# Moving the SBUF tiles of a clustered-attention and MLP kernel by up to 608 bytes

## Chip, cores and metric

The kernel runs on one core of one Trainium2 chip. The metric is the device time of one execution in microseconds (us); the median of three runs of the kernel before is 843.01 us (842.73 to 843.17).

## What is computed

The reference is an attention with a mask by cluster, followed by two MLPs. All arrays are float32.

```python
q_assign = argmax(einsum('bhsd,hcd->bhsc', q_n, c_n), -1)   # likewise k_assign, 16 clusters
mask = q_assign[:, :, :, None] == k_assign[:, :, None, :]
scores = where(mask, scale * q @ k.T, -1e9)
x = softmax(scores) @ v                    # batch 2, heads 8, sequence 768, head dim 64
x = x.transpose(0, 2, 1, 3).reshape(1536, 512)
h = x @ w_in                               # 512 -> 2048
x = where(h > 0, h, exp(min(h, 0)) - 1) @ w_out          # 2048 -> 512
return ((x @ w_a) * (x @ w_b)) @ w_out2    # 512 -> 1536 -> 512
```

## The kernel before, in words

**Order.** The order of all work is written out by hand in the string ORDER; each word names a small function (an op) and its arguments, and every engine runs its share in that order. The first 270 us are mostly attention, the next 40 us a mixture, and the rest is MLP alone.

**Attention.** For each of 16 heads (batch times heads) and each of six tiles of 128 queries, `sc` (L671) makes the scores in PSUM with float32r matmuls of 384 columns: two with `qa`/`ka` (128 rows, the float32 values in two parts) and two with `qb`/`kb` (80 rows, 16 of which carry the mask). `rm` (L679, VectorE) takes the maximum, `ex` (L690, ScalarE) the exponential into `pf` and its row sums into `sum`. `tr` (L723) transposes `pf` on TensorE with `pf` as stationary operand and the identity `identf` as moving one; `th` and `tl` cut the result into two float16 parts in `pt`, or POOL's `hi` and `lo` and a transposing DMA `td` do. `av` (L782) multiplies `pt` with the float16 parts `v1`, `v2` of v. `ra`, `rc`, `rx`, `rb` (L742, L747, L753, L763) spread the reciprocal of the row sums with `identf` as moving operand. `sm` (L571) makes the similarities to the centroids from `cq1`, `ck1`, `ck2`, `cq2`, and `st` (L585) transposes them from `sim`.

**MLP.** The 1536 tokens go in three chunks c of 512, the hidden width in blocks blk of 512. Every product of two float32 matrices is three float32r matmuls of 128 rows, 128 stationary and 512 moving columns (`mm3`, L921 to L923): high by high, high by low, low by high part. There are four kinds of op, each of 24 such matmuls (the very last `o` is cut in two of 12):

- `h:blk.c.fp`, 24 ops (4 blocks, 3 chunks, 2): weights `w[2 blk]` stationary, `x_c` moving.
- `x2:blk.c.dp`, 24 ops: weights `w[2 blk + 1]` stationary, the activation `g` moving.
- `ab:blk.c.ft`, 36 ops (3 blocks, 3 chunks, 4): weights `w[8 + 3 blk]` for 12 matmuls, then `w[9 + 3 blk]` for 12, stationary; `x_c` moving.
- `o:blk.c.jp`, 18 ops: `g` stationary, weights `w[10 + 3 blk]` moving.

That makes 102 ops and 2448 matmuls. Each matmul has its own weight load (PEld), which starts with the matmul before it. VectorE's `gl` (L992) and `pl` (L1039) write the low part of `g` that `x2` and `o` need. POOL's `wq` (L907) writes the last part of each weight tile.

**Where tiles lie.** SBUF is filled from two ends: pools opened with `left(...)` grow upward, pools with `right(...)` downward from the top. A tile takes its bytes per partition, rounded up to 32, and tiles of a pool lie in the order of their creation. Weight tile `w[i]` goes to pool `w(i % 4)`; the activation tile of step u = 3 blk + c (counted on over the four `h` blocks and the three `ab` blocks) goes to `gA` for even and `gB` for odd u. In the compiled program the MLP's operands begin at these places, all tiles being multiples of 512 bytes long:

| tiles | side | first byte | modulo 512 |
|---|---|---|---|
| w0 | left | 50176 | 0 |
| x0 | left | 66560 | 0 |
| w1 | left | 82944 | 0 |
| gA | left | 107520 | 0 |
| x1 | left | 123904 (to 140288) | 0 |
| x2 | right | 155616 (to 172000) | 480 |
| gB | right | 180192 | 480 |
| w2 | right | 196576 | 480 |
| w3 | right | 212960 (to 229344) | 480 |

In the attention (modulo 512): `qa`, `ka`, `qb`, `kb` 224; `pf`, `pt` 416; `v1`, `v2` 416 or 160; `rx` 480; `identf` 160; `cq1` and its like 352; `sim` 96; `identb` 0. `sum` and `rs` take 32 bytes a buffer, two buffers each; `desc` takes 64 and `ohscale` 32.

The lines that the change touches are L294 (the first right-hand pool), L310 to L316 (the constants), L688 (`sum`) and L741 (`rs`).

Of the kernel before, what the change touches and what calls it, by code (L numbers as in the profile page):

```python
# [10 lines left out]
F32 = mybir.dt.float32  # L11
# [10 lines left out]
P = 128  # L22
B, H, S, D, C = 2, 8, 768, 64, 16
# [232 lines left out]
def clustered_attention_moe_kernel(  # L256
# [21 lines left out]
    def left(name, reuse="tile", under=ctx):  # L278
        return under.enter_context(tc.tile_pool(name=name, bufs=1, reuse_waits=reuse))

    def right(name, under, reuse="tile"):
        return under.enter_context(
            tc.tile_pool(name=name, bufs=1, side="right", reuse_waits=reuse)
        )

    const = left("const")
# [4 lines left out]
    wp = left("wp")  # L291
    ectx, actx, actxA, actxB = ExitStack(), ExitStack(), ExitStack(), ExitStack()
    ep = left("prep", under=ectx)
    ap = right("attn", actx)  # L294
    spB = right("operandsB", actxB)
    sp = [right("operandsA", actxA), spB]
# [2 lines left out]
    def take(pool, tag, shape, dt, name, bufs=1):  # L299
        return pool.tile(shape, dt, tag=tag, bufs=bufs, name=name)  # L300
# [6 lines left out]
    identb = ep.tile([P, P], BF16, name="identb")  # L307
    warm = ep.tile([P, 512], BF16, name="warm")
    nc.vector.memset(warm, 0.0)
    eps = const.tile([P, 1], F32, name="eps")  # L310
    nc.vector.memset(eps, 1e-9)
    identf = const.tile([P, P], F32, name="identf")
    make_identity(nc, identf)
    desc = ep.tile([P, C], F32, name="desc")
    ones = ep.tile([NH, P], F32, name="ones")
    ohscale = ep.tile([64, 2], F32, name="ohscale")  # L316
    cn = ep.tile([P, D], F32, name="cn")
    nc.sync.dma_start(out=cn, in_=cent)
    csq = ep.tile([P, D], F32, name="csq")
# [156 lines left out]
    pairs = [{} for _ in range(NPAIR)]  # L476

    def flat(t):
        return t.rearrange("p t d -> p (t d)")
# [203 lines left out]
    @op  # L683
    def ex(g, t):
        j, x = divmod(g, 2)
        f, a = divmod(t, 3)
        if (x, a) == (0, 0):
            pairs[j]["sum", f] = take(ap, "sum", [P, 2, 3], F32, f"sum_{j}_{f}", 2)  # L688
        pf = st[g][f"pf{t}"] = take(ap, "pf", [P, S], F32, f"pf{t}_{g}", 3)
        nc.scalar.activation(  # L690
            pf.rearrange("p (a b) -> p a b", a=2), st[g].pop(f"sc{t}")[:, :, :HALF], AF.Exp,
            bias=st[g].pop(f"nm{t}"), accum_out=pairs[j]["sum", f][:, x, a : a + 1],
        )
# [44 lines left out]

    @op
    def ra(j, f):  # L740
        s = pairs[j]["rs", f] = take(ap, "rs", [P, 6], F32, f"rs_{j}_{f}", 2)  # L741
        nc.scalar.activation(s, flat(pairs[j]["sum", f]), AF.Identity, bias=eps)  # L742

    @op
# [345 lines left out]
    for word in ORDER.split():  # L1090
        name, args = word.split(":")
# [45 lines left out]
```

## Time and profile before

| | |
|---|---|
| median of three runs | 843.01 us |
| span of the profiled execution, first to last instruction | 842.1 us |
| TensorE busy in the span | 823.9 us, 98% |
| VectorE, ScalarE, POOL busy | 609.5, 408.3, 357.5 us |
| granted TensorE clock | 1.00 in every stretch |

The profiled execution's own time is not told beside its span; the span is 0.9 us under the median of the runs. A matmul's end is modelled in these records, its start is not: two matmuls overlap in the table of busy time, so the pace of TensorE is read from start to start.

### The profile page before, as it was taken

How to read it: one execution, taken by the hardware profiler on the slowest of the kernel's cores; microseconds unless marked ns; L12 is line 12 of the kernel's file. 1: busy time of each engine (PE TensorE's matmuls, PEld its weight loads, DVE VectorE, ACT ScalarE, POOL GpSimd, SP SyncE). 2: the span in 40 equal slices, each digit the busy share in tenths (PEclk: the TensorE clock that was granted, in tenths of full speed). 3: DMA queues.
4: the chain of work that ended last, by engine and by line, in shares of the span. 5: the costliest groups of instructions: out<-in, count | busy, mean ns of one | idle time of the engine just before them, and what ended most of it. 6: DMA issues, size and time to landing. Idle time of an engine off the chain costs nothing.

```text
span 842.1 us, 12217 instructions
## 1 busy us (share of the span) xinstructions
PE 823.9 (98%) x4626; PEld 656.1 (78%) x4626; DVE 609.5 (72%) x871; ACT 408.3 (48%) x730; POOL 357.5 (42%) x307
## 2 busy tenths in 40 slices
PE   9899999999999999999999999999999999999998
PEld 8777666776667888888888888888888888888886
DVE  5898998899889879698687688776247874455222
ACT  6687877877787644454454365342122332222020
POOL 3666776687472325354444443332034440422000
PEclk9999999999999999999999999999999999999999
DMA  9446655666343212222222222113002221110102
GB/s 280 111 91 147 134 100 108 132 126 105 65 86 64 75 58 69 75 76 94 82 89 82 80 76 76 51 50 100 1 3 97 61 85 56 51 51 0 51 1 100
DMA packets 65626, 68.12 MB, mean 81 GB/s; under 512 B 49888, under 2 KB 49888, under 8 KB 65568
## 3 DMA queue, kind: packets, MB, share of 16 engines
q1 hardware_dynamic: 65328, 66.76, 30.6%
q8 instruction: 36, 0.59, 0.3%
q10 hardware_dynamic: 240, 0.59, 0.3%
q14 instruction: 22, 0.18, 0.1%
HBM read 48.27 MB, written 3.15 MB: 61 GB/s over the span
## 4 chain that ended last, share of the span: by engine, by line
PE 90%; DVE 4%; POOL 3%; ACT 2%; issue 2%; POOLq 0%; ACTq 0%; DVEq 0%
PE ab L923 8%; PE ab L922 8%; PE ab L921 8%; PE sc L671 6%; PE h L921 5%; PE h L923 5%; PE h L922 5%; PE x L923 5%; PE x L921 5%; PE x L922 5%; PE av L782 4%; PE o L923 4%; PE o L921 4%; PE o L922 4%; PE tt L723 4%; PE sm L571 4%
## 5 line engine op out<-in xcount | busy, mean ns | idle before, releaser
L679 DVE TENSOR_REDUCE nm<-sc 128x1 f32<-128x768 f32 x96 | 90.9, 950 | 14.3 <-PE sc L671 13.6
L690 ACT ACTIVATE pf<-sc,nm 128x768 f32<-128x768 f32 x96 | 86.8, 905 | 21.0 <-DVE nm L679 13.2
L1023 ACT COPY t0ab<-ab 128x512 f32<-128x512 f32 x36 | 21.1, 587 | 113.7 <-PE ab L923 113.7
L732 DVE TENSOR_TENSOR pt<-tt,pt 128x384 f16<-128x384 f32 x132 | 69.3, 547 | 5.5 <-ACT pt L727 5.1
L1028 DVE TENSOR_TENSOR t1ab<-ab,t0ab 128x512 f32<-128x512 f32 x36 | 24.8, 689 | 66.0 <-ACT t0ab L1023 65.9
L727 ACT CAST pt<-tt 128x384 f16<-128x384 f32 x126 | 57.3, 479 | 25.8 <-PE tt L723 24.3
L671 PE MATMUL sc<-ka,qa 128*128 128x384 f32 x192 | 58.2, 384 | 7.1 <-ACT pf L690 6.5
L723 PE MATMUL tt<-identf,pf 128*128 128x128 f32 x396 | 60.3, 277 | 4.1 <-DVE pt L732 2.0
L723 PEld LDWEIGHTS tt<-identf,pf 128*128 128x128 f32 x396 | 45.7, 140 | 15.1 <-issue 4.3
L782 PE MATMUL av<-pt,v 128*64 128x384 f16 x576 | 54.0, 329 | 0.0
L852 ACT ACTIVATE wg<-wraw 128x512 f32<-128x512 f32 x68 | 45.1, 667 | 17.9 <-DMA wraw<-in_w_out_dram 7.2
L705 POOL TENSOR_TENSOR phl<-pf,phl 128x768 f16<-128x768 f32 x30 | 50.9, 1696 | 4.7 <-issue 1.9
L869 DVE SCALAR_TENSOR_TENSOR wf<-wraw,wg 128x512 int32<-128x512 int32 x68 | 51.2, 753 | 1.9
L882 DVE SCALAR_TENSOR_TENSOR wg<-wraw,wg 128x512 f32<-128x512 uint32 x68 | 49.7, 731 | 1.8
L671 PE MATMUL sc<-kb,qb 80*128 80x384 f32 x192 | 49.5, 339 | 0.0
L1039 DVE TENSOR_TENSOR gl<-t1ab,gh 128x512 fp32r<-128x512 f32 x36 | 33.8, 940 | 18.8 <-ACT gh L1034 18.6
L857 DVE TENSOR_SCALAR wg<-wg 128x512 f32<-128x512 f32 x68 | 40.1, 590 | 6.4 <-ACT wg L852 6.4
L671 PEld LDWEIGHTS sc<-ka,qa 128*128 128x128 f32 x192 | 28.8, 189 | 19.8 <-ACT pf L690 13.6
L782 PEld LDWEIGHTS <-v 128*64 128x64 f16 x576 | 29.7, 109 | 17.6 <-issue 6.9
L862 DVE TENSOR_SCALAR wg<-wg 128x512 int32<-128x512 int32 x68 | 41.8, 615 | 2.1
L698 POOL CAST phl<-pf 128x768 f16<-128x768 f32 x26 | 23.5, 903 | 43.9 <-ACT pf L690 42.9
L992 DVE TENSOR_TENSOR gl<-t1h,gh 128x1024 fp32r<-128x1024 f32 x24 | 33.9, 1414 | 7.7 <-ACT gh L985 7.7
(388 smaller groups left out, 2349.0 us busy)
## 6 DMA issues: line engine op xcount, KB each, us to landing
wraw<-in_w_out_dram SPq DMA_DIRECT2D x28, 512.0 KB, 3.3
wraw<-in_w_in_dram SPq DMA_DIRECT2D x16, 512.0 KB, 3.7
wraw<-in_w_a_dram SPq DMA_DIRECT2D x12, 512.0 KB, 3.6
wraw<-in_w_b_dram SPq DMA_DIRECT2D x12, 512.0 KB, 3.4
rawq<-in_qt_dram SPq DMA_DIRECT2D x30, 192.0 KB, 3.6
acc<-in_v_dram SPq DMA_DIRECT2D x4, 768.0 KB, 11.1
rawk<-in_kt_dram SPq DMA_DIRECT2D x15, 192.0 KB, 3.7
kb<-ka SPq DMA_DIRECT2D x14, 192.0 KB, 3.0
```

The costliest lines, as they stand in the source:

```text
L671: nc.tensor.matmul(s[:, j, :HALF], a[:, qs], b[:, j * HALF : (j + 1) * HALF], start=i == 0, stop=i == 1,)
L679: nc.vector.reduce_max(out=nm, in_=st[g][f"sc{t}"][:, :, :HALF], axis=AX.XY, negate=True)
L690: nc.scalar.activation(pf.rearrange("p (a b) -> p a b", a=2), st[g].pop(f"sc{t}")[:, :, :HALF], AF.Exp, bias=st[g].pop(f"nm{t}"), accum_ou ...
L705: nc.gpsimd.tensor_sub(phl[:, S:], st[g].pop(f"pf{t}"), phl[:, :S])
L723: nc.tensor.transpose(tt[:, k * P : (k + 1) * P], pf[:, o : o + P], identf)
L727: (nc.vector.tensor_copy, nc.scalar.copy)[e](next(parts_of(g, t, u)), st[g][f"tt{t}{u}"])
L732: nc.vector.tensor_sub(lo, st[g].pop(f"tt{t}{u}"), hi)
L782: nc.tensor.matmul(pairs[j]["av"][x * 64 : (x + 1) * 64].rearrange("p (a q) -> p a q", a=3), st[2 * j + x][("v1", "v2")[vi]][:, kt_, :], s ...
L869: nc.vector.scalar_tensor_tensor(out=f, in0=raws[n][:, :, 1], scalar=-0x40000000, in1=g, op0=ALU.bitwise_and, op1=ALU.bitwise_or,)
L921: nc.tensor.matmul(ps, lhi, rhi, start=first, stop=False)
L922: nc.tensor.matmul(ps, lhi, rlo, start=False, stop=False)
L923: nc.tensor.matmul(ps, llo, rhi, start=False, stop=last)
```

## The change

A new pool, opened first on the right, holds one tile of 120 float32 (480 bytes) that nothing reads or writes. `identf` is created ahead of `eps`. `desc` is created twice as wide and used by half, `ohscale` with 16 columns instead of 2, `sum` and `rs` with 16 instead of 6. No instruction is added, removed or moved.

```diff
+    edge = right("edge", ctx).tile([P, 120], F32, name="edge")
     ap = right("attn", actx)
...
+    identf = const.tile([P, P], F32, name="identf")
     eps = const.tile([P, 1], F32, name="eps")
     nc.vector.memset(eps, 1e-9)
-    identf = const.tile([P, P], F32, name="identf")
     make_identity(nc, identf)
-    desc = ep.tile([P, C], F32, name="desc")
+    desc = ep.tile([P, 2 * C], F32, name="desc")[:, :C]
     ones = ep.tile([NH, P], F32, name="ones")
-    ohscale = ep.tile([64, 2], F32, name="ohscale")
+    ohscale = ep.tile([64, 16], F32, name="ohscale")
...
-            pairs[j]["sum", f] = take(ap, "sum", [P, 2, 3], F32, f"sum_{j}_{f}", 2)
+            pairs[j]["sum", f] = take(
+                ap, "sum", [P, 16], F32, f"sum_{j}_{f}", 2
+            )[:, :6].rearrange("p (x a) -> p x a", x=2)
...
-        s = pairs[j]["rs", f] = take(ap, "rs", [P, 6], F32, f"rs_{j}_{f}", 2)
+        s = pairs[j]["rs", f] = take(ap, "rs", [P, 16], F32, f"rs_{j}_{f}", 2)[:, :6]
```

## Rows read from the trace of the kernel before

**Rows 1.** The page: busy time by engine, TensorE's granted clock in 40 slices.
```profile
PE 823.9 (98%) x4626; PEld 656.1 (78%) x4626; DVE 609.5 (72%) x871; ACT 408.3 (48%) x730; POOL 357.5 (42%) x307
...
PEclk9999999999999999999999999999999999999999
```

**Rows 2.** The page: the chain of work that ended last, by engine.
```profile
PE 90%; DVE 4%; POOL 3%; ACT 2%; issue 2%; POOLq 0%; ACTq 0%; DVEq 0%
```

**Rows 3.** Who TensorE's matmuls waited for, whole span: total us, times, longest.
```profile
PE sc L671 <- ACT pf L690: 6.5, 9, 1.4
PE tt L723 <- DVE pt L732: 2.0, 4, 1.0
PE vbc L460 <- DVE vdg L453: 1.7, 1, 1.7
PE warm_ps L407 <- DVE eps L311: 1.2, 1, 1.2
PE tt L723 <- ACT pf L690: 1.2, 1, 1.2
...
PE op L626 <- DVE oht L617: 0.2, 1, 0.2
```

**Rows 4.** Timeline, TensorE, weights left, moving left: start us, us, engine, line.
```profile
412.99 0.39 PE L921 MATMUL h<-x0h,w4h 128*128 128x512 f32 x1
...
439.97 0.39 PE L923 MATMUL x<-gh,w5l 128*128 128x512 f32 x1
```

**Rows 5.** Timeline, TensorE, weights right, moving right.
```profile
374.52 0.39 PE L921 MATMUL h<-x2h,w2h 128*128 128x512 f32 x1
...
385.17 0.39 PE L923 MATMUL h<-x2h,w2l 128*128 128x512 f32 x1
```

**Rows 6.** Timeline, TensorE, weights right, moving left.
```profile
341.21 0.39 PE L921 MATMUL h<-x0h,w2h 128*128 128x512 f32 x1
...
363.38 0.40 PE L923 MATMUL h<-x1h,w2l 128*128 128x512 f32 x1
```

**Rows 7.** Timeline, TensorE, weights left, moving right.
```profile
440.19 0.40 PE L921 MATMUL h<-x2h,w4h 128*128 128x512 f32 x1
...
462.36 0.40 PE L923 MATMUL x<-gh,w5l 128*128 128x512 f32 x1
```

**Rows 8.** Timeline, TensorE, one `ab` op and the next: weights w11 right, w12 left.
```profile
650.15 0.39 PE L921 MATMUL ab<-x0h,w11h 128*128 128x512 f32 x1
...
652.95 0.39 PE L921 MATMUL ab<-x0h,w12h 128*128 128x512 f32 x1
...
655.67 0.39 PE L921 MATMUL ab<-x0h,w11h 128*128 128x512 f32 x1
```

**Rows 9.** Timeline, TensorE: first matmul of the unbroken MLP run and the last.
```profile
297.02 0.39 PE L921 MATMUL x<-gh,w1h 128*128 128x512 f32 x1
...
838.04 0.39 PE L923 MATMUL o<-w16h,gl 128*128 128x512 f32 x1
```

**Rows 10.** Groups by form, attention's matmuls: busy us, mean ns, idle before.
```profile
L723 PE MATMUL tt<-identf,pf 128*128 128x128 f32 x396 | 60.3, 277 | 4.1 <-DVE pt L732 2.0 <-ACT pf L690 1.2 <-ACT ohs L631 0.5
...
L763 PE MATMUL rbp<-identf,rx 128*128 128x128 f32 x96 | 13.6, 278 | 0.1
...
L571 PE MATMUL sm<-qa,cq 128*64 128x384 f32 x32 | 12.3, 385 | 0.2 <-DVE pt L732 0.2
```

**Rows 11.** By line: VectorE's product of `ab`, ns min/median/max over both sides' tiles.
```profile
L1028 DVE TENSOR_TENSOR t1ab<-ab,t0ab x36: 677/692/693, 546.1 to 817.0; 128x512 f32<-128x512 f32 x36
```

**Rows 12.** Timeline, VectorE: the last `gl` ahead of the `x2` of step 1.2.
```profile
393.86 1.22 DVE L992 TENSOR_TENSOR gl<-t1h,gh 128x1024 fp32r<-128x1024 f32 x1
```

**Rows 13.** Timeline, TensorE: the first matmul that reads that half of `gl`.
```profile
398.23 0.39 PE L922 MATMUL x<-gl,w3h 128*128 128x512 f32 x1
```

**Rows 14.** Timeline, POOL: the last two pieces of w15, then TensorE's first use.
```profile
733.35 2.55 POOL L907 TENSOR_TENSOR w15l<-wf,wg 128x512 fp32r<-128x512 f32 x2
...
741.96 0.39 PE L923 MATMUL ab<-x0h,w15l 128*128 128x512 f32 x1
```

## The prediction

> **What bounds the kernel now.** I read the page first. [...] So the question is where TensorE waits and how fast it goes when it does not. The waits of its matmuls are nine entries, all of the start or the attention: none names a line of the MLP (L921 to L923) [rows 3]. From 297.02 us, where the attention's last interruptions of `h` are over, to the last matmul's start at 838.04 us TensorE therefore runs one unbroken stream [rows 9]. By the program it holds all but the first four `h` ops, 2448 - 96 = 2352 matmuls, hence 2351 intervals: 541.02 / 2351 = 230.1 ns each. Anything that changes this pace goes straight to the end.
>
> The third view is the timeline of TensorE, read from start to start, sorted by the side of SBUF on which the two operands lie:
>
> - weights left, moving left: 120 matmuls, 26.98 us / 119 = 226.7 ns [rows 4];
> - weights right, moving right: 48 matmuls, 10.65 / 47 = 226.6 ns [rows 5];
> - weights right, moving left: 96 matmuls, 22.17 / 95 = 233.4 ns [rows 6];
> - weights left, moving right: 96 matmuls, 22.17 / 95 = 233.4 ns [rows 7].
>
> There are two paces only. [...] It is not the op, the weights or the chunk: inside one `ab` op, with `x0` moving throughout, the 12 matmuls with the right-hand w11 take 2.80 / 12 = 233.3 ns each and the next 12 with the left-hand w12 2.72 / 12 = 226.7 ns [rows 8].
>
> In the table of places left-hand operands begin at 0 modulo 512 and right-hand ones at 480, and all slices of them are multiples of 512 bytes. So a matmul is fast when the two addresses agree modulo 512, whatever their common value, and slow when they differ by 32 bytes.
>
> **The change part by part.** *The edge tile.* It is the first right-hand pool, so it lies on top and pushes all below it down by 480 bytes. The MLP pool follows directly: x2, gB, w2, w3 go from 480 to 0 modulo 512. Nothing of the left changes there, since the constants keep their sum and the pools behind `prep` start where `prep` starts. Every MLP pair then agrees.
>
> How many are dear now is counted from the code. `h`: even blocks have w0, dear with chunk 2; odd blocks w2, dear with chunks 0 and 1: 2 x 1 + 2 x 2 = 6 pairs of block and chunk, 12 ops. `x2`: one chunk of each block disagrees (step u of the other parity than the block): 4 pairs, 8 ops. `ab`: block 0 (w0, w1) with chunk 2, 4 ops; block 1 (w3, w0) half of each of 12 ops, worth 6; block 2 (w2, w3) with chunks 0 and 1, 8 ops; 18 in all. `o`: weights of w2, w1, w0 against g: 2 + 2 + 1 chunks, 10 ops. That is 48 ops of 24, 1152 of 2448 matmuls, 1152 x 6.67 ns = 7.7 us. From the whole run it is 541.02 - 2351 x 0.2267 = 8.0 us; the 0.3 us between the two are the matmuls just after a switch, which reach the fast pace late. With no switches left they go too, so I take **8.0 us**, with 7.7 as the lower value.
>
> *Does the faster stream stay unbroken?* Its suppliers must be early enough. `x2` and `o` need the last `gl` or `pl`; the tightest of the 21 heads is the `x2` of block 1, chunk 2: `gl` ends at 393.86 + 1.22 = 395.08 us [rows 12], the matmul that reads it starts at 398.23 us [rows 13], 3.1 us later. In between lies about one op, which shrinks by at most 24 x 6.67 = 0.16 us. Among the weights w15 is near: written at 733.35 + 2.55 = 735.90 us, first used at 741.96 us, 6.1 us [rows 14]; some 60 matmuls lie between the VectorE work that lets it go on and its use, 0.4 us of shrinking. Cost 0; what covers it is those margins, and if the `gl` cover were gone each head would pay the lateness itself. VectorE's own operations do not care: the 36 products of `ab`, half with scratch on each side, lie within 677 to 693 ns [rows 11].
>
> *The rounded small tiles and identf* act in the attention only. Edge, `rs` and `sum` together move `pf`, `pt`, `v1`, `v2` to 32 bytes less modulo 512 (416 to 384, 160 to 128), and `qa`, `ka`, `qb`, `kb` to 96 less (224 to 128); `rx` goes from 480 to 0. `identf` goes from 160 to 128. On the left `desc` and `ohscale` push `cq1` and its like from 352 to 448 and `sim` from 96 to 192. What counts by the rows above is the difference of a pair, and it stays for `sc` (0), for `tr` (416 - 160 = 256, then 384 - 128) and for `av`. It changes for 96 records of `rb` (320 to 384), 128 matmuls of `sm` (multiples of 128, then 64 past them) and 48 of `st`, 272 in all. The trace of before cannot show what the new differences cost, so the bound on both sides is the only step seen, 272 x 6.67 ns = 1.8 us. The nearest row is the transpose, whose difference is 256 and which takes 277 ns where `rb` takes 278 [rows 10]: one nanosecond, 0.1 us for all `rb`. I take 0. In the attention TensorE also has waits that take up such a gain or loss [rows 3]. `edge` issues nothing and no queue is touched: no instruction, DMA or wait is added on any engine.
>
> *Order of reuse.* Tiles wait for the earlier tiles in whose bytes they lie. Left moves by +96 and right by -480 to -608 bytes against each other; adding the sizes up, every MLP tile lies over the same attention tiles as before (`ohs` now ends on the byte where gA begins). Cost 0; otherwise `x2`'s parts, written while the attention ends, would be late.
>
> **Sum.** 842.1 - 8.0 = 834.1 us of span. The end behind the last matmul stays. The median of the runs is 0.9 us above the span, so 835.0 us. The bounds: 833.2 with all 272 attention matmuls gaining, 837.1 with all losing and 7.7 us for the MLP.
>
> **The rivals.** *A. Sides, not offsets: no change, 843.0 us.* In the trace of before offset and side go together, so the dear pairs could be those whose operands lie in two different regions. Then equal offsets give nothing. Against it: x1 ends at 140288 and x2 begins at 155616, and left-hand tiles from 50176 to 140288 pair well with each other, as do right-hand ones from 155616 to 229344 [rows 4, 5]; a border would have to fall into those 15 KB. Distance does not do it either: w0 and x1 are fast over 74 KB [rows 4], x1 and w2 slow over 73 KB [rows 6]. Chance 0.05.
> [...]
>
> *B. The shift does not come out equal: 843.0 us.* If the edge were not the topmost tile or not of 480 bytes after rounding, left and right would differ by another number. 480 is a multiple of 32 and the pool is the first on the right. Chance 0.03.
>
> *C. TensorE outruns its suppliers: slower.* Place: the 21 heads of `x2` and `o`. To end more than 0.2% slower, waits would have to eat 8.0 us and 1.7 more, 9.7 / 21 = 0.46 us at every head, beyond margins of 3.1 us and more; the result would be 844.7 us or above. It decides where a head's `gl` comes over 3.1 us later, relative to TensorE, than now. VectorE is 72% busy [rows 1], the shrinking per op is 0.16 us. Chance 0.02.
>
> *D. Half the gain: 838 to 841 us,* if the agreed pairs that I did not see (right at 0 with left at 0) behaved like neither group, or the attention paid more than its bound. Left with left at 0 is exactly rows 4. Chance 0.05.
>
> **How the numbers follow.** The forecast's own case, every MLP matmul at 226.7 ns and the attention as it is, has 0.85: 835.0 us. With D's 0.05 faster has 0.90; A and B make 0.08 for the same, C 0.02 for slower. The range is the forecast's bounds, 833.2 to 837.1 us; the rest left out is about 0.15, so no rival has to be taken in. 0.2% of 843 us, 1.7 us, is about what a measurement of this kernel can tell from no change.
>
> **What would show it.** In the changed kernel every stretch of MLP runs at 226.7 ns from start to start, also the counterparts of rows 6, 7 and both halves of rows 8; the run from the first `x2` to the last matmul takes 533 us; the waits of TensorE still name no MLP line; the first `x2` still starts near 297 us, within 2 us. The prediction is wrong if mixed pairs still take 233.3 ns (A, B), if L921 to L923 appear among the waiting lines (C), or if the MLP starts later than 299 us.

## The result

The kernel after takes 835.36 us (median of six runs, 834.66 to 838.53) against 843.09 us (842.73 to 846.54): a ratio of 0.9902, 95% interval 0.9881 to 0.9922. The profiled execution has a span of 833.1 us, 9.0 us less than before.

The page and the waits come first (the line numbers are four higher than before, L925 to L927 are `mm3`).

The page of the kernel after, busy time by engine:

```profile
PE 815.0 (98%) x4626; PEld 655.3 (79%) x4626; DVE 609.9 (73%) x871; ACT 408.4 (49%) x730; POOL 357.4 (43%) x307
```

Its waits of TensorE's matmuls, again nine entries, of which the longest and the last:

```profile
PE sc L673 <- ACT pf L694: 6.5, 9, 1.4
...
PE op L628 <- DVE oht L619: 0.2, 1, 0.2
```

As many instructions as before, the same busy times on VectorE, ScalarE and POOL to 0.4 us, the same waits. Only TensorE's busy time fell, by 8.9 us. Where, the timeline of TensorE tells (start us, us, engine, line): the unbroken MLP run [rows 9], the mixed pairs [rows 6, 7] and the `ab` op with w11 and w12 [rows 8].

```profile
296.19 0.39 PE L925 MATMUL x<-gh,w1h 128*128 128x512 f32 x1
...
339.71 0.39 PE L925 MATMUL h<-x0h,w2h 128*128 128x512 f32 x1
...
361.24 0.39 PE L927 MATMUL h<-x1h,w2l 128*128 128x512 f32 x1
...
437.63 0.39 PE L925 MATMUL h<-x2h,w4h 128*128 128x512 f32 x1
...
459.16 0.39 PE L927 MATMUL x<-gh,w5l 128*128 128x512 f32 x1
...
644.35 0.39 PE L925 MATMUL ab<-x0h,w11h 128*128 128x512 f32 x1
...
647.07 0.39 PE L925 MATMUL ab<-x0h,w12h 128*128 128x512 f32 x1
...
649.79 0.39 PE L925 MATMUL ab<-x0h,w11h 128*128 128x512 f32 x1
...
829.08 0.39 PE L927 MATMUL o<-w16h,gl 128*128 128x512 f32 x1
```

The whole run takes 532.89 us for its 2351 intervals, 226.7 ns each, where it took 541.02. Weights right with moving left is now 21.53 / 95 = 226.6 ns (233.4 before), weights left with moving right the same, and both halves of the `ab` op take 2.72 us for 12. So 8.13 of the 9.0 us come from the MLP. The run starts 0.83 us earlier, at 296.19 instead of 297.02 us, and the end behind the last matmul is 4.0 us in both (833.1 - 829.08, 842.1 - 838.04).

The 0.83 us were there before the attention began. Busy time of TensorE in the stretch from 4 to 8 us (us, busy, matmuls, granted clock, DMA share, GB/s), before and then after:

```profile
4.00:8.00 4.00, 4.00 (x51) 1.00 1.03 222
```

```profile
4.00:8.00 4.00, 4.00 (x66) 1.00 1.03 223
```

These are the warm-up matmuls of `wm`, which depend on nothing of the change. In the timeline 51 of them run at 106 ns start to start in the profiled execution before and 35 in the one after, until the pace becomes 56 ns; 16 x 50 ns = 0.8 us. All of them have one shape, 128 columns, so up to 6.7 us in the one execution and 5.0 us in the other TensorE ran at about half its later pace, although the clock column shows 1.00 for both: it does not tell the two apart, and the 1.00 in every stretch, in the table of before, does not speak for these first microseconds. Between this and the MLP the two executions stay within 0.1 us of each other: the attention gained and lost nothing.

### The profile page after: what moved, and what is told of

Same layout as the page of the kernel before. It is cut to its first block, busy times and chain, and to the rows that moved or that the text cites. A ratio compares the mean times of both kernels' runs of the same rounds, so it can differ in the third digit from the quotient of the medians.

```text
span 833.1 us, 12217 instructions
## 1 busy us (share of the span) xinstructions
PE 815.0 (98%) x4626; PEld 655.3 (79%) x4626; DVE 609.9 (73%) x871; ACT 408.4 (49%) x730; POOL 357.4 (43%) x307
## 4 chain that ended last, share of the span: by engine, by line
PE 89%; DVE 3%; POOL 3%; ACT 2%; issue 2%; DMA 0%; SPq 0%; POOLq 0%; ACTq 0%; DVEq 0%
PE ab L926 8%; PE ab L925 8%; PE ab L927 8%; PE sc L673 6%; PE h L925 5%; PE h L927 5%; PE x L927 5%; PE h L926 5%; PE x L926 5%; PE x L925 5%; PE av L786 4%; PE o L926 4%; PE o L925 4%; PE o L927 4%; PE tt L727 4%; PE sm L573 4%
```

## The experiments

The theory to test was the prediction's: a 512-column matmul takes 6.67 ns more when the address of its moving operand and that of the weights loaded beside it differ modulo 512. Its rivals: it is the multiple of 512 that counts, not the agreement; some other period than 512 counts; and the attention's matmuls pay or do not. [rows 8] show the slow and fast halves of `ab` change with the stationary operand alone. That it is the weights loaded beside the matmul, the next one's (in the trace of before each load of the run starts 2 to 4 ns after the matmul ahead of its own), and not its own, the same trace shows where an agreeing pair is followed by another pair. There are 22 such places where the next pair disagrees in itself. The last agreeing matmul is slow, 235 ns to the next start, in the 16 where its moving operand disagrees with the next weights, and fast, 226 to 227 ns, in the 6 where it agrees with them.

For the attention the choice is between two values. If each of its 620 matmuls whose difference the edge tile alone makes an odd multiple of 32 bytes (396 transposes, 128 of `sm`, 96 of `rb`) paid the 6.67 ns of [rows 8], that would be up to 4.1 us, and a transpose would start 116 ns after the one before it where it now takes 109. If only the 512-column stream pays, the attention stays as it is.

### The edge tile alone, and all but the edge tile

```diff
+    edge = right("edge", ctx).tile([P, 120], F32, name="edge")
     ap = right("attn", actx)
```

> The 480-byte tile alone; small tiles and identf stay as before. The MLP's operands all begin at 0 modulo 512, so every theory expects its stream at 226.7 ns and the MLP 8.1 to 8.2 us shorter. In the attention the pairs now differ by an odd multiple of 32 bytes: transposes 160 against 448 (288), sm 352 against 256 (96), rb 160 against 0 (352). [...]

Measured 834.8 us (834.64 to 835.61), ratio to before 0.9893, interval 0.9874 to 0.9912: the kernel after, within its interval. Timeline of TensorE, the MLP run:

```profile
296.12 0.39 PE L922 MATMUL x<-gh,w1h 128*128 128x512 f32 x1
...
829.01 0.39 PE L924 MATMUL o<-w16h,gl 128*128 128x512 f32 x1
```

532.89 us again. And the transposes, by line (ns min/median/max), whose operands differ by an odd multiple of 32 bytes here and by 256 in the kernel after, which follows:

```profile
L724 PE MATMUL tt<-identf,pf x396: 270/273/332, 36.6 to 275.7; 128*128 128x128 f32 x198
```

```profile
L727 PE MATMUL tt<-identf,pf x396: 270/273/332, 36.6 to 275.7; 128*128 128x128 f32 x198
```

Not a nanosecond. These durations rest on modelled ends, but the starts agree: in the traces of before, after and the edge alone a transpose starts 109 ns after the one before it in the median, and an `rb` matmul 112 ns. The intervals within `sm` add up to 27.40, 27.43 and 27.44 us, so `sm` and `rb` did not pay either. The second value stands: the 512-column stream pays and these attention matmuls do not, and the rounded small tiles and `identf` are worth nothing.

The other half has the diff of the change without its `edge` line.

> Small tiles and identf moved, without the 480-byte tile. Right-hand MLP operands stay at 480, so both theories expect mixed pairs at 233.3 ns and the MLP as before. In the attention the differences become 224 for transposes (352 against 128), 352 for sm and 352 for rb. Theory 'every matmul pays': 843.0 plus up to 4.1, 844 to 847 us. Rival 'only the 512-column stream pays': 843.0 us, within 0.5.

Measured 844.0 us, ratio 1.0008, interval 0.9994 to 1.0023: no change. The timeline has the MLP run at

```profile
299.46 0.39 PE L924 MATMUL x<-gh,w1h 128*128 128x512 f32 x1
...
840.48 0.39 PE L926 MATMUL o<-w16h,gl 128*128 128x512 f32 x1
```

541.02 us as before. Its start is 2.4 us later than in the profile of before. The granted clock fell for a moment near 91 and 256 us (its mean is 0.99 up to 120 us and 0.96 from 240 to 280 us, 1.00 in the other stretches), where 14 `av` intervals take 313 to 320 ns instead of 159; the two dips cost 1.6 and 1.5 us, and the warm-up ended 0.7 us earlier. It is no cost of the layout: three of the 17 runs of the kernel before that were taken beside this one have the same mean clock, 0.996, and take 846.5 to 846.7 us.

### Both sides at 480

```diff
+    wpad = wp.tile([P, 120], F32, name="wpad")
+    epad = ep.tile([P, 8], F32, name="epad")
```

> No edge tile; instead 480 bytes ahead of the left-hand weight pool (and 32 more ahead of the prep pool, so that the attention keeps its differences). All MLP operands begin at 480 modulo 512, none at a multiple of 512. Theory 'the two addresses have to agree': all of the MLP at 226.7 ns, 835.0 us. Rival 'operands have to begin at multiples of 512': no pair is right, nothing better than before, 843.0 us (or 233.3 ns throughout, 851 us).

Measured 835.74 us (834.81 to 838.48), ratio 0.9913, interval 0.9891 to 0.9934. The MLP run in its timeline:

```profile
296.12 0.39 PE L923 MATMUL x<-gh,w1h 128*128 128x512 f32 x1
...
829.01 0.39 PE L925 MATMUL o<-w16h,gl 128*128 128x512 f32 x1
```

532.89 us, with no operand of the MLP at a multiple of 512. Agreement counts; the multiple does not.

### Which differences cost

In the kernel after, unused tiles between the right-hand MLP tiles:

```diff
+    pads = {"gh": 16, "w2h": 32, "w3h": 40, "end": 24}
+    def pad(pool, tag):
+        if pool is pools.get("gB") and tag in pads:
+            pool.tile([P, pads.pop(tag)], F32, name=f"pad_{tag}")
...
+        pad(pool, tag)
...
+        if tag == "w3l":
+            pad(pool, "end")
```

> After, with unused tiles between the right-hand MLP tiles so that x2 begins at 64, gB at 128, w2 at 256, w3 at 416 modulo 512 and the left side stays at 0: pairs that differ by 64, 96, 128, 160, 192, 224 and 256 bytes. Theory 'agreement modulo 512': every pair but the equal ones takes 233.3 ns or more, about 843 us or above. Rival 'agreement modulo 64': 64, 128, 192, 256 at 226.7 ns, 96, 160, 224 at 233.3 ns, 837 to 840 us. Third: a pace below 226.7 ns at some difference, which would be a faster layout still.

One run, 842.32 us. Timeline, first and last matmul of two or four ops: x2 with w0 (difference 64), gB with w1 (128), x0 and x1 with w2 (256), x2 with w2 (320), gA with w3 (96); differences are modulo 512:

```profile
306.87 0.40 PE L935 MATMUL h<-x2h,w0h 128*128 128x512 f32 x1
...
317.64 0.39 PE L937 MATMUL h<-x2h,w0l 128*128 128x512 f32 x1
317.87 0.40 PE L935 MATMUL x<-gh,w1h 128*128 128x512 f32 x1
...
328.80 0.39 PE L937 MATMUL x<-gh,w1l 128*128 128x512 f32 x1
...
339.95 0.39 PE L935 MATMUL h<-x0h,w2h 128*128 128x512 f32 x1
...
361.49 0.40 PE L937 MATMUL h<-x1h,w2l 128*128 128x512 f32 x1
...
372.91 0.40 PE L935 MATMUL h<-x2h,w2h 128*128 128x512 f32 x1
...
383.68 0.39 PE L937 MATMUL h<-x2h,w2l 128*128 128x512 f32 x1
...
383.91 0.40 PE L935 MATMUL x<-gh,w3h 128*128 128x512 f32 x1
...
394.89 0.39 PE L937 MATMUL x<-gh,w3l 128*128 128x512 f32 x1
```

64: 10.77 / 47 = 229.1 ns. 128: 10.93 / 47 = 232.6. 256: 21.54 / 95 = 226.7. 320: 10.77 / 47 = 229.1, as for 64. 96: 10.98 / 47 = 233.6. The expectation of modulo 512 falls with the 256, that of modulo 64 with the 128. In these pairs the pace repeats after 256 bytes (256 as agreement, 320 as 64), and within them the loss is not the same everywhere. No difference was faster than agreement.

A second sweep cut the right-hand tiles out of larger ones, a few bytes from their start:

```diff
+    first = {"x2": 16, "gB": 8, "w2": 64, "w3": 4}
...
+        t = pool.tile([P, 2048 + 128], dt, tag=tag, bufs=bufs, name=name)
+        return t[:, by : by + 2048].rearrange("p (a b) -> p a b", a=4)
```

> After, with right-hand MLP tiles cut out of larger ones so that x2 begins 16, gB 8, w2 64 and w3 4 bytes past a multiple of 512; left at 0: differences of 4, 8, 12, 16, 56, 48 and 64 bytes in either direction. Theory 'the loss grows with the distance from the next multiple of 256 bytes' (0: 226.7, 64: 228.7, 128: 232.5, but 32: 233.3 in the kernel before): it can't say much below 32. Theory 'equal place within a line of some bytes': 4, 8, 12, 16 already cost up to 6.7 ns. Rival 'a line of 32 bytes or more is read as one': 4 to 16 cost nothing. Also looked for: any pace below 226.7 ns.

One run, 843.93 us. Timeline: x2 with w0 (16), x0 and x1 with w2 (-64, moving minus stationary), gB with w3 (4), and x2 with w11, which lies in the place of w3 (12; half an `ab` op, 12 matmuls):

```profile
306.80 0.39 PE L933 MATMUL h<-x2h,w0h 128*128 128x512 f32 x1
...
317.69 0.40 PE L935 MATMUL h<-x2h,w0l 128*128 128x512 f32 x1
...
340.01 0.40 PE L933 MATMUL h<-x0h,w2h 128*128 128x512 f32 x1
...
362.18 0.39 PE L935 MATMUL h<-x1h,w2l 128*128 128x512 f32 x1
362.41 0.39 PE L933 MATMUL x<-gh,w3h 128*128 128x512 f32 x1
...
373.41 0.40 PE L935 MATMUL x<-gh,w3l 128*128 128x512 f32 x1
...
700.20 0.39 PE L933 MATMUL ab<-x2h,w11h 128*128 128x512 f32 x1
...
702.70 0.39 PE L935 MATMUL ab<-x2h,w11l 128*128 128x512 f32 x1
```

16: 10.89 / 47 = 231.7 ns. -64: 22.17 / 95 = 233.4, where +64 had 229.1. 4: 11.00 / 47 = 234.0. 12: 2.50 / 11 = 227 ns, and in the other seven groups of this pair the pace is 226.7 as well, but for the first four intervals of one, just behind a slow pair. Four bytes already cost as much as 32, so the rival with a line of 32 bytes is out, and the sign matters. Twelve bytes cost nothing: agreement is fast, but it is not the only difference that is, and the loss does not grow with the distance from it. Again no group has a pace below 226.7 ns.

### An edge of 224 bytes

If 256 is the period, right-hand operands may begin at 256 while left-hand ones begin at 0.

```diff
-    edge = right("edge", ctx).tile([P, 120], F32, name="edge")
+    edge = right("edge", ctx).tile([P, 56], F32, name="edge")
```

> After with an edge tile of 224 bytes instead of 480: right-hand MLP tiles begin at 256 modulo 512, left ones at 0. Theory 'agreement modulo 256 is enough' (the sweep had 226.7 ns for pairs 256 apart): all of the MLP at 226.7 ns and 835 us as the kernel after. Rival 'agreement modulo 512, the sweep's pairs were fast for another reason': mixed pairs at 233.3 ns, 843 us.

Measured 835.7 us, ratio 0.9902, interval 0.9881 to 0.9923, the ratio of the kernel after. The MLP run:

```profile
299.63 0.39 PE L925 MATMUL x<-gh,w1h 128*128 128x512 f32 x1
...
832.52 0.39 PE L927 MATMUL o<-w16h,gl 128*128 128x512 f32 x1
```

532.89 us, 226.7 ns an interval. Agreement modulo 256 is enough here.

### Why the attention does not pay

In the kernel after, 32 bytes between `ka`/`kb` and `qa`/`qb` of the even pairs of heads, and between `v1`/`v2` and `pt`:

```diff
+    shifts = {"pt": ap, "qa1": sp[0]}
...
+        if shifts.get(tag) is pool:
+            shifts.pop(tag).tile([P, 8], F32, name=f"pad_{tag}")
```

> After, with 32 unused bytes between ka/kb and qa/qb of the even pairs of heads only (the odd pairs are the control), and 32 between v1/v2 and pt. Even pairs: scores matmuls (384 columns, float32r) differ by 32 bytes; all av matmuls (384 columns, float16) differ by 32. [...] Rival 'only 512 columns pay' (as the 128-column transposes of the edge-only kernel paid nothing): both halves equal, av 159 ns. The MLP stays at 226.7 ns.

One run, 835.81 us. From the timeline, the three intervals inside the 48 scores groups of the even pairs: medians 261, 174 and 177 ns with 32 bytes of difference, against 260, 174 and 179 ns for the same groups in the kernel after. The odd pairs, without a difference, have 279, 175 and 179, and 279, 174 and 179. `av` by line, first with 32 bytes of difference, then the kernel after:

```profile
L790 PE MATMUL av<-pt,v x576: 326/326/350, 61.9 to 285.8; 128*64 128x384 f16 x192
```

```profile
L786 PE MATMUL av<-pt,v x576: 326/326/350, 60.9 to 284.9; 128*64 128x384 f16 x192
```

Start to start the mean over `av` is 77.7 ns in both (two matmuls of a pair start 3 to 4 ns apart). The attention pays nothing: with 6.67 ns more, the scores of the even pairs would have gone from 174 to 181 ns. In the scores the moving operand lies 32 bytes below the stationary one; the other direction was not tried there. Is it the 384 columns, or the short groups of four? Two kernels with the layout of before, whose MLP matmuls move fewer columns in the inner 10 of 12 (the products of the columns left out are missing from the result):

```diff
-        nc.tensor.matmul(ps, lhi, rlo, start=False, stop=False)
+        nc.tensor.matmul(cut(ps, False), lhi, cut(rlo, False), start=False, stop=False)
...
```

> The kernel before (mixed pairs 32 bytes apart), but of the 12 MLP matmuls of a group the inner 10 move only the first 384 of 512 columns; the products of the other 128 columns are left out there. Weight loads are as before (188 ns each in the records). [...] Rival 'a steady stream always pays and the scores escaped because their groups are only four long': 174 ns agreeing, 180 to 181 ns mixed.

Timeline, the second and the eleventh matmul of a group, for w4 with x1 (both left), w2 with x1 (difference +32) and w4 with x2 (-32):

```profile
405.53 0.34 PE L925 MATMUL h<-x1l,w4h 128*128 128x384 f32 x1
...
407.11 0.33 PE L925 MATMUL h<-x1l,w4h 128*128 128x384 f32 x1
...
340.99 0.34 PE L925 MATMUL h<-x1l,w2h 128*128 128x384 f32 x1
...
342.58 0.34 PE L925 MATMUL h<-x1l,w2h 128*128 128x384 f32 x1
...
423.21 0.34 PE L925 MATMUL h<-x2l,w4h 128*128 128x384 f32 x1
...
424.78 0.34 PE L925 MATMUL h<-x2l,w4h 128*128 128x384 f32 x1
```

Nine intervals take 1.58, 1.59 and 1.57 us: 175.6, 176.7 and 174.4 ns (the medians over all such groups are 175.3, 177.0 and 173.7). The mixed pairs lose 1.7 ns in one direction and gain 1.7 in the other. So a steady stream of 384 columns does not lose 6.7 ns, and the rival with 180 is out; but one common pace of 174 for pairs that agree and pairs that do not is not it either, since agreement is not the best.

> The same with 448 of 512 columns in the inner 10 matmuls. [...] Rival 'the loss grows with the number of columns': 200 and about 205.8 ns. [...]

The same two matmuls of a group in the timeline:

```profile
410.29 0.36 PE L925 MATMUL h<-x1l,w4h 128*128 128x448 f32 x1
...
412.11 0.36 PE L925 MATMUL h<-x1l,w4h 128*128 128x448 f32 x1
...
349.37 0.37 PE L925 MATMUL h<-x1l,w2h 128*128 128x448 f32 x1
...
351.23 0.37 PE L925 MATMUL h<-x1l,w2h 128*128 128x448 f32 x1
```

1.82 and 1.86 us, 202.2 and 206.7 ns; the medians are 202.8 with agreement, 206.7 at +32 and 204.4 at -32. The mixed value at +32 is 0.9 ns over the expected 205.8, the agreeing one 2.8 ns over the expected 200, which was the author's estimate; no run shows it. A loss of the whole 6.67 ns fails, and so does the 5.8 ns between those two numbers: the loss at +32 and -32 is 3.9 and 1.7 ns here, 6.7 and 6.7 with 512 columns, 1.7 and -1.7 with 384. What it does depend on is the number of columns and the direction, and why is not settled by these runs.

## Why the prediction was right

That the pace depends on the two places holds, and so does the size, about 8 us. That the time, 835.36 us, comes as near as 0.4 us to the predicted 835.0 is partly luck, as the sum below shows. Step by step:

- **The pace of the agreeing pairs.** Predicted 226.7 ns everywhere, 533 us for the run; measured 226.7 ns and 532.89 us. The term of the MLP, 8.0 us, came out as 8.13. Of the two ways of counting it the one over the whole run was right; the trace of before shows why: its 1152 disagreeing matmuls (the dear ones) take 233.26 ns on average, 7.59 us over the fast pace, and 81 agreeing ones beside a switch lose another 0.53 us, 65 of them behind it, as the prediction has it, and 16 just ahead of one. The 6.67 ns a matmul of the count are the step inside [rows 8], 2.80 - 2.72 us over 12 matmuls; over all 1152 the step is 233.26 - 226.67 = 6.6 ns.
- **No new wait.** TensorE's waits name no MLP line, as forecast. The margins at the heads were not used up.
- **The attention at 0.** Right, and for a wider reason than was given. The prediction let the changed differences of `sm`, `rb` and `st` cost or gain up to 1.8 us; the edge-only kernel has odd multiples of 32 bytes in `sm`, `rb` and the transposes and shows that they cost nothing (109 and 112 ns from start to start as before, `sm` 27.44 us against 27.40).
- **The sum.** The span fell by 9.0 us instead of 8.0: 0.83 us are the warm-up's start, which the layout does not govern, the rest is the 0.13 us above. The median rose above that span by 2.3 us where 0.9 had been added: the profiled execution itself took 834.88 us, 1.8 us over its span. The 0.9 us were no fixed cost but the distance of one profiled execution before from the median of others; with the same 1.8 us it took about 843.9 us, an estimate. So the forecast had the span 1.0 us too long and what lies above it 1.4 us too short, and the two errors nearly cancel.
- **The rivals.** A and B are out: the mixed pairs are fast although they lie on two sides. C did not come: no wait. D did not come: the pairs of a right-hand tile at 0 with a left-hand one at 0 take the same 226.7 ns.

One step was right only as far as it went. "Fast when the two addresses agree modulo 512" was read from two differences, 0 and 32; 256 bytes apart is as fast, as the edge of 224 bytes shows (532.89 us), and so is a difference of 12 bytes (226.7 ns). And the multiple of 512 that the change aims at is not needed, as both sides at 480 show. Of the change's parts only the edge tile works; the others are worth nothing here. In this kernel the places of the two operands decide whether a matmul takes 226.7 or 233.3 ns, 8.1 us in all; no run shows where the 6.67 ns go.

## What to carry to other kernels

In a long stream of float32r matmuls of 512 columns, each with its own weight load, lay out moving and stationary tiles so that their byte addresses agree modulo 256; here that was worth 6.7 ns, 3%, of every matmul whose operands were 32 bytes off, and an unused tile of 224 or 480 bytes at the edge of a side was enough. Other differences cost between nothing (226.7 ns at 12 bytes) and over 7 ns (234.0 at 4), in no simple order, and none was faster. Before trying it, sort the start-to-start intervals of the stream by the two operands' places: two sharp groups, here 226.7 and 233.4 ns, mean that the gain can be counted beforehand. The short groups of the attention, transposes and float16 products showed no difference here, and with 384 columns agreement, 175.3 ns, lies between the two directions, 173.7 and 177.0.

## What the runs showed that was not expected

Four bytes of difference cost as much as 32 (234.0 ns against 233.4), twelve cost nothing, and +64 costs 2.4 ns where -64 costs 6.7. With 384 columns a difference of -32 bytes is 1.7 ns faster than agreement.

The granted clock can dip for a few microseconds in the attention, in one execution and not in the next. Two stretches of the kernel with the edge of 224 bytes (busy us, matmuls, clock, DMA share, GB/s), and then of the kernel after:

```profile
87.00:91.00 4.00, 2.65 (x20) 0.98 0.17 35
90.00:95.00 5.00, 5.00 (x31) 0.66 0.75 162
```

```profile
87.00:91.00 4.00, 2.65 (x21) 1.00 0.18 37
90.00:95.00 5.00, 5.00 (x48) 1.00 0.75 163
```

31 matmuls instead of 48 at a granted clock of 0.66 instead of 1.00, with `av` at 313 ns from start to start instead of 160. Ahead of it TensorE had waited, a good microsecond of it for `pf`, and was busy in 2.65 of the 4 us from 87 on. But the kernel after was busy as long there and kept its clock, so what decides between the two is not shown. A second dip, near 256 us, is alike: the clock is 0.65 in 256 to 259 us, and TensorE was busy in 2.41 of the 4 us from 251 on. With both dips and the warm-up's start this execution has a span of 836.5 us instead of 833.1, which is the size of the scatter between runs of one kernel.
